# Four reorderings in a fused attention and feed-forward kernel: the start, one weight load, one output group, and the moment at which the next loads begin

## Chip, cores and metric

The kernel runs on one core of a Trainium2 chip. The metric is the device time of one execution in microseconds (us). A time is given as the median of several executions; a ratio is the mean time of one kernel's fast executions over the mean of the fast executions of the kernel before, taken in the same rounds on the same chip, so it is not quite the ratio of the medians quoted beside it. On one core an execution counts as slow when it is over 1.5% above the fastest of the same kernel.

Engine names as in the profile: PE is TensorE, DVE is VectorE, ACT is ScalarE, POOL is GpSimd, SP is SyncE. PEld is TensorE's loading of weights; SPq, ACTq and PEq are the engines' instruction queues; all DMAs of the page's list of issues come from SP's and POOL's. The span is the time from the first to the last instruction. The granted clock is the share of TensorE's full clock that the profile records as granted to it. POOL issues the loads from HBM that convert float32 to bfloat16; SP issues the DMA transposes and the stores.

## The reference, cut

```python
# q, k, v: [4, 8, 768, 64]; every row sees the first 8 keys and its last 96 keys
scores = q @ k^T / sqrt(64) - slope[h] * dist        # masked outside those keys
a = softmax(scores);  x = (a @ v) as [3072, 512]     # tokens x (heads * 64)
h = x @ w_in                                         # w_in  [512, 2048]
g = s * relu(h)**2 + b
out = g @ w_out                                      # w_out [2048, 512], float32 out
```

## The kernel before

The 3072 tokens are worked in 12 granules of 256. For granule `j`, `SS` computes scores and probabilities, `A` the attention output `xn[j]`, a transpose turns it into `xT[j]`, `P1` multiplies with `w_in` (8 groups of 8 matmuls) and `P2` with `w_out`. From granule 3 on everything is one software pipeline: period `j` holds the attention of `j`, `P1` of `j-1` and `P2` of `j-2` and `j-1`, and it loads granule `j+2`.

```python
    def pace(j):                       # POOL reads one element: its loads wait for it
        nc.gpsimd.tensor_copy(pdum[:], pts[j, 0][0:1, 0, 0:1])

    def load_granule(j):               # 2 + 2 + 2 DMAs of 128 KB, rows of 256 B in HBM
        load_rows(j, "k"); load_rows(j, "q"); load_v(j)

    def XT_dma(j):                     # two DMA transposes, 128 tokens each
        xT[j] = xpool.tile([P, KC, GT], BF16, name="xT", tag="xT")
        for i in range(GB):
            nc.sync.dma_start_transpose(xT[j][:, :, i * P : (i + 1) * P],
                                        xn[j][:, i, :, :].rearrange("p h d -> p (h d)"))
    # ... (cut)
    def period(j, items, at, late=None):
        SS(j, (0, 1))
        if j + 2 < NJ:
            pace(j)
            load_granule(j + 2)
        run(items, at[0])              # items: P1(j-1,0), P2(j-2,4), P1(j-1,1), ...
        A(j, 0)
        # ... (cut: A(j,1), SS(j,(2,3)), A(j,2), A(j,3) with items between)
        if late is None:
            XT_dma(j)                  # x transposes, then
        if j + 2 < NJ:
            XB(j + 2)                  # four transposes of k and q, on the same SP queue
        run(items, 100)                # the rest of P1 and P2
```

In the traces POOL's instructions run in the order of the program, and it has nothing else to do in the pipeline, so the tensor that `pace` reads, and not its place in the program, decides when the six loads begin (the timelines below show it: the copy after a wait of 10.63 us in before, then the loads 0.3 to 0.4 us after it). In before that is the first probabilities of granule `j`.

At the start, the first k and q arrive as float32 in two halves each (`raw32`, loaded by SP), are cast by DVE and ACT and transposed on PE. A POOL copy from `raw32` holds all of POOL's loads until the first k half has landed (in before it runs at 3.82 us, and the first v load follows at 4.20).

The softmax here doesn't subtract the row's maximum and nothing guards it: scores larger than these inputs give would overflow.

## Time and profile before

| | before |
|---|---|
| median of 4 executions, us | 219.19 (218.12 to 219.5) |
| profiled execution, us (span) | 223.86 (222.0), a slow one |
| PE busy | 95% of the span |
| one period, granules 4 to 6, us | 16.15 and 15.85 |
| x transpose, issue to landing, us | median 2.5, longest 5.8 |

The page of before: busy us of each engine, then the chain of work that ended last, by engine.

```profile
PE 210.5 (95%) x2027; PEld 141.7 (64%) x2027; DVE 135.8 (61%) x322; ACT 115.9 (52%) x176; POOL 69.1 (31%) x93
PE 74%; DMA 15%; DVE 4%; SPq 3%; ACT 2%; issue 1%
```

PE bounds the kernel, so time can only come from PE's idle time. The view of waits lists it: who waited for whom, us in total, times, longest.

```profile
PE ps L487 <- DMA xT<-xn: 2.1, 1, 2.1
PE ps_s L369 <- DMA qT<-qnat: 1.3, 1, 1.3
PE ps_t L263 <- DVE knat L155: 1.1, 1, 1.1
...
PE ps_t L263 <- DVE qnat L155: 0.5, 1, 0.5
```

The first line is a single stall, at 117 us. The chain in order of time (start, us, what) shows it: the x transpose of granule 6 took 5.65 us.

```profile
112.23 1.19 SPq L467
113.47 5.65 DMA xT<-xn
119.25 1.03 PE ps L487 x8
```

A usual period looks different. These are the timelines of SP, of POOL and of PE in before (start, us, engine, line, operation, out<-in, count).

```profile
80.23 2.50 SPq L467 DMA_TRANSPOSE xT<-xn  x2
82.82 2.52 SPq L294 DMA_TRANSPOSE kT<-knat  x2
```

```profile
86.94 0.18 POOL L124 COPY pdum<-pt 1x1 bf16<-1x1 bf16 x1 [10.63 <-DVE pt L386]
87.48 1.75 POOL L103 DMA_DIRECT2D knat<-in_k_dram  x2 [0.36 <-issue]
```

```profile
98.12 2.75 PE L530 MATMUL ps<-w_out_bf,gT 128*128 128x512 bf16 x12
100.81 0.51 PE L369 MATMUL ps_s<-qT,kT 64*128 64x128 bf16 x12
101.25 1.05 PE L487 MATMUL ps<-xT,w_in_bf 128*128 128x256 bf16 x8
```

The x transposes are issued at 80.23 and about 81.5 us and land 2.4 us after issue; the loads of the next granule start 7 us after the first of them; PE reaches the first P1 that needs them about 4.9 us after the first issue (here 101.25 for those issued at 96.38). The second transpose therefore has a slack of 1.1 to 1.2 us: it could land that much later before PE waits.

### The profile page before, as it was taken

The page shows a single profiled execution, that of the slowest core. Times are in us where ns is not written, and L with a number is a line of the kernel's source. Part 1 is how long each engine was busy: PE and PEld are TensorE (multiplying, and loading weights), DVE is VectorE, ACT ScalarE, POOL GpSimd, SP SyncE. Part 2 cuts the span into 40 slices and gives each one's busy share as a digit, 9 for nine tenths or more (in the row PEclk, how much of TensorE's full clock was granted, in tenths as well). Part 3 has the DMA queues.
Part 4 walks back from the last instruction along what each step waited for, and adds up shares of the span by engine and source line. Part 5 has one row for each costly group of instructions (what it writes and reads, how often), then busy time and mean ns, then how long its engine had stood idle before and what let it go on. Part 6 is the DMA issues. An engine that isn't in the chain of part 4 may idle for free.

```text
span 222.0 us, 4984 instructions
## 1 busy us (share of the span) xinstructions
PE 210.5 (95%) x2027; PEld 141.7 (64%) x2027; DVE 135.8 (61%) x322; ACT 115.9 (52%) x176; POOL 69.1 (31%) x93
## 2 busy tenths in 40 slices
PE   7779999999799999999996999999999999999993
PEld 2346877446566766766753676775776676675763
DVE  4565657699689676655754394664675675652431
ACT  6558899534557545544534445645544644641430
POOL 6966563450462702704505400810900000000000
PEclk9999999999999999999998899999999999999999
DMA  5999999999899996995997934995995322022102
GB/s 160 143 166 195 187 192 206 163 127 137 89 126 254 108 127 101 165 167 79 200 150 92 182 65 95 134 156 107 131 162 101 70 73 73 0 75 70 47 3 95
DMA packets 107207, 27.60 MB, mean 124 GB/s; under 512 B 95792, under 2 KB 104240, under 8 KB 107184
## 3 DMA queue, kind: packets, MB, share of 16 engines
q0 software_dynamic: 72896, 13.11, 80.6%
q1 hardware_dynamic: 34288, 14.17, 30.7%
q8 instruction: 16, 0.26, 0.5%
q14 instruction: 7, 0.06, 0.1%
HBM read 27.26 MB, written 6.29 MB: 151 GB/s over the span
## 4 chain that ended last, share of the span: by engine, by line
PE 74%; DMA 15%; DVE 4%; SPq 3%; ACT 2%; issue 1%
PE ps L487 32%; PE ps L530 28%; DMA knat<-in_k_dram 6%; PE ps_av L414 5%; PE ps_s L369 5%; DMA qT<-qnat 4%; DMA xT<-xn 3%; DMA raw<-in_k_dram 2%; PE ps_2e L581 2%; PE ps_2s L530 2%; SPq L294 1%; ACT gT L496 1%; DVE xn L423 1%; PE ps_s L353 1%; SPq L302 1%
## 5 line engine op out<-in xcount | busy, mean ns | idle before, releaser
L487 PE MATMUL ps<-xT,w_in_bf 128*128 128x256 bf16 x768 | 95.4, 274 | 2.6 <-DMA xT<-xn 2.1
L496 ACT ACTIVATE gT<-ps 128x512 bf16<-128x512 f32 x96 | 57.3, 598 | 62.6 <-PE ps L487 62.1
L487 PEld LDWEIGHTS <-w_in_bf 128*128 128x128 bf16 x768 | 73.6, 98 | 21.1 <-issue 3.6
L530 PE MATMUL ps<-w_out_bf,gT 128*128 128x512 bf16 x336 | 83.4, 381 | 0.0
L478 DVE TENSOR_TENSOR gT<-gT 128x512 bf16<-128x512 bf16 x96 | 39.9, 420 | 25.6 <-ACT gT L496 25.6
L382 ACT ACTIVATE pt<-ps_s 128x1024 bf16<-128x1024 f32 (+1 forms) x48 | 43.2, 952 | 21.0 <-PE ps_s L369 20.7
L530 PEld LDWEIGHTS <-gT 128*128 128x128 bf16 x368 | 33.7, 98 | 30.5 <-issue 0.3
L386 DVE TENSOR_TENSOR pt<-pt,tmpl 128x1024 bf16<-128x1024 bf16 (+1 forms) x40 | 26.1, 653 | 14.6 <-ACT pt L382 13.6
L124 POOL COPY pdum<-pt 1x1 bf16<-1x1 bf16 x7 | 1.7, 237 | 72.5 <-DVE pt L386 72.5
L111 POOL DMA_DIRECT2D vaug<-in_v_dram x24 | 21.5, 913 | 3.7 <-DMA w_out_bf<-in_moe_w_out_dram 3.0
L423 DVE TENSOR_TENSOR xn<-ps_av,rc 128x256 bf16<-128x256 f32 x48 | 20.4, 424 | 1.7
L541 DVE SCALAR_TENSOR_TENSOR o_sb<-ps,s_bc,bvec 128x512 f32<-128x512 f32 x18 | 13.5, 748 | 12.6 <-PE ps L530 12.6
L414 PEld LDWEIGHTS <-pt 128*128 128x128 bf16 x352 | 16.2, 98 | 6.7 <-DVE xn L423 2.3
L422 DVE RECIPROCAL rc<-ps_av 128x4 f32<-128x4 f32 x48 | 8.6, 180 | 16.8 <-PE ps_av L414 16.5
L414 PE MATMUL ps_av<-vaug,pt 128*128 128x65 bf16 x224 | 17.7, 194 | 0.6 <-DVE rc L422 0.3
L103 POOL DMA_DIRECT2D knat<-in_k_dram x18 | 15.8, 883 | 6.3 <-PE ps_av L414 1.9
L103 POOL DMA_DIRECT2D qnat<-in_q_dram x18 | 15.9, 897 | 0.8 <-issue 0.8
L369 PE MATMUL ps_s<-qT,kT 64*128 64x128 bf16 x224 | 12.6, 218 | 1.4 <-DMA qT<-qnat 1.3
L414 PE MATMUL ps_av<-vo,pt 128*128 128x65 bf16 x128 | 12.2, 195 | 0.0
L369 PEld LDWEIGHTS <-kT 64*128 64x128 bf16 x224 | 7.1, 94 | 7.6 <-issue 6.9
L369 PE MATMUL ps_s<-qT,ko 64*128 64x128 bf16 x128 | 8.0, 216 | 0.0
L530 PE MATMUL ps_2s<-w_out_bf,gT 128*128 128x512 bf16 x32 | 7.6, 379 | 0.0
(67 smaller groups left out, 105.1 us busy)
## 6 DMA issues: line engine op xcount, KB each, us to landing
out_dram<-o_sb SPq DMA_DIRECT2D x23, 256.0 KB, 3.0
vaug<-in_v_dram POOLq DMA_DIRECT2D x24, 128.0 KB, 6.1
knat<-in_k_dram POOLq DMA_DIRECT2D x18, 128.0 KB, 4.9
qnat<-in_q_dram POOLq DMA_DIRECT2D x18, 128.0 KB, 6.0
w_in_bf<-in_moe_w_in_dram POOLq DMA_DIRECT2D x8, 256.0 KB, 10.5
w_out_bf<-in_moe_w_out_dram POOLq DMA_DIRECT2D x4, 512.0 KB, 12.7
raw<-in_k_dram SPq DMA_DIRECT2D x2, 256.0 KB, 3.9
raw<-in_q_dram SPq DMA_DIRECT2D x2, 256.0 KB, 4.2
```

Source lines behind the costliest of these rows:

```text
L103: nc.gpsimd.dma_start(t[:, i, :, :], src[b, :, sb * P : (sb + 1) * P, :].rearrange("h p d -> p h d"))
L111: nc.gpsimd.dma_start(vaug[b][:, sb, :, 0:D], v[b, :, sb * P : (sb + 1) * P, :].rearrange("h p d -> p h d"),)
L369: nc.tensor.matmul(ps[:, hi, oc * P : (oc + 1) * P], lhsT=kt[r, :], rhs=qT[j][r, hp, i * P : (i + 1) * P], start=not biased, stop=not bias ...
L382: nc.scalar.activation(pt[:, :, 0:n], ps[:, :, 0:n], ACT.Exp, scale=QSCALE)
L386: nc.vector.tensor_tensor(pt[:, :, 0:n], pt[:, :, 0:n], m, ALU.mult)
L414: nc.tensor.matmul(av[:, i, hi, :], lhsT=pt[:, hi, c * P : (c + 1) * P], rhs=vv, start=n_ == 0, stop=n_ == len(ops) - 1,)
L423: nc.vector.tensor_tensor(xn[j][:, :, 2 * hp : 2 * hp + 2, :], av[:, :, :, 0:D], rc[:].to_broadcast((P, GB, 2, D)), ALU.mult,)
L478: nc.vector.tensor_tensor(gs, gs, gs, ALU.mult)
L487: nc.tensor.matmul(ps[:, i, :], lhsT=w_in_bf[:, kc, fc * P : (fc + 1) * P], rhs=xT[j][:, kc, :], start=(kc == 0), stop=(kc == KC - 1),)
L496: nc.scalar.activation(gs, ps[:], ACT.Relu)
L530: nc.tensor.matmul(po[j, tb], lhsT=gT[j][:, fc, tb * P : (tb + 1) * P], rhs=w_out_bf[:, fc, :], start=(fc == 0), stop=(fc == FC - 1),)
L541: nc.vector.scalar_tensor_tensor(out=o_sb[:], in0=po[j, tb], scalar=s_bc[:], in1=bvec[:], op0=ALU.mult, op1=ALU.add,)
```

## The change

The intent: shorten the start, bring the k rows of granule 3 forward, and start each granule's loads earlier so that they are over before the next x transposes.

```diff
     def pace(j):
-        nc.gpsimd.tensor_copy(pdum[:], pts[j, 0][0:1, 0, 0:1])
+        nc.gpsimd.tensor_copy(pdum[:], xn[j - 1][0:1, 0, H - 1, 0:1])
@@ start of POOL's loads
-    nc.gpsimd.tensor_copy(pdum[:], raw32[0:1, 0, 0, 0:1])
     load_v(0)
@@ more_loads
+        load_rows(3, "k")
         load_w_out(3)
-        load_rows(3, "k")
@@ start: scores 0 and 1 before the second key half
-    idle(1, "av")
+    idle(2, "av")
+    for hp in range(2):
+        S_mm(0, hp, True)
+        S_post(0, hp, True)
     T_mm(0, 1, "k")
# ... (cut: SB_mm(0, 2) and SB_mm(0, 3) one step earlier)
@@ x of granule 0 before q of granule 1
+    XT_half(0, 1, "dve", "av")
     T_mm(1, 0, "q")
-    XT_half(0, 1, "dve", "av")
# ... (cut: P1(0, 3), P1(0, 4), P1(0, 5) earlier, between A and x of granule 1)
# ... (cut: P2 of granule 1 before the last P2 parts of granule 0, so that
#      w_out's last quarter may land later)
@@ period
-        SS(j, (0, 1))
         if j + 2 < NJ:
             pace(j)
             load_granule(j + 2)
+        SS(j, (0, 1))
```

More of the change, by code (lines that the diff above doesn't have):

```diff
@@ L623 @@
     cast("q", 1)
-    for hp in range(2):
-        S_mm(0, hp, True)
-        S_post(0, hp, True)
     idle(1, "av")
+    SB_mm(0, 2)
     T_mm(0, 1, "q", "av", True)
@@ L631 @@
     more_loads()
-    SB_mm(0, 2)
+    SB_mm(0, 3)
     S_mm(0, 2, True)
@@ L635 @@
     A(0, 0, "pso")
-    SB_mm(0, 3)
     S_mm(0, 3, True)
@@ L673 @@
     A(1, 2)
+    P1(0, 3)
     A(1, 3, "pso")
-    P1(0, 3)
     XT_half(1, 0, "act", "av")
+    P1(0, 4)
     XT_half(1, 1, "dve", "pso")
-    P1(0, 4)
+    P1(0, 5)
     P1(1, 0)
@@ L682 @@
     P1(1, 2)
-    P1(0, 5)
     make_tmpl(3)
@@ L721 @@
     XB(4)
+    P2_sc(1, 0, 0)
+    P2_mm(1, 0, 0)
     wsum_part(0)
+    XT_pe(2, "act", "psh")
+    P2_mm(1, 0, 1)
+    wsum_part(1)
+    P2_mm(1, 0, 2)
     P2_mm(0, 0, 3)
-    XT_pe(2, "act", "psh")
-    wsum_part(1)
     P2_raw(0, 0)
+    wsum_part(2)
     P2_mm(0, 1, 3)
     P2_raw(0, 1)
-    wsum_part(2)
-    P2_sc(1, 0, 0)
-    for part in range(4):
-        P2_mm(1, 0, part)
+    P2_mm(1, 0, 3)
     P2_raw(1, 0)
```

## The prediction

In item 6 of the prediction a sentence on how the queues share the DMA engines is cut, since no run here shows it; the transpose's 5.9 us beside loads against 2.5 alone carry the item without it. The sum loses no term: it is -0.8, -0.3, -1.3 and +0.7 us as recorded (they add up to -1.7; the record says about -1.9).

> **What bounds the kernel.** TensorE. The page has PE busy 210.5 of 222.0 us (95%), with 74% of the chain of work that ended last; from 60 us on the timeline is nearly gapless, one period of about 16.1 us per granule. So only PE's idle time can be saved. The profiled execution is a slow one (223.9 us against 219.15): PE waited 2.1 us at 117 us for an x transpose (5.8 us to landing instead of 2.5), and the windows then show the granted clock at 0.65 and 0.50 for 4 us. Such a stall costs about 4.5 us (estimate: 223.9 - 219.15); I take it as absent from the usual run.
>
> The rest of PE's idle time: in the first 16 us gaps of 0.35, 1.06 (k half 1), 0.46 (q half 1), 0.72 (kT evacuation) and 0.43 us (qT evacuation), 0.35 us at 22.7 (last A of granule 1), and 1.28 us at 55.4 us (qT of granule 3).
>
> **Behind the start: the load stream.** From the DMA view: w_in part 0 lands at 15.5 us (first P1 starts 16.2), part 2 at 21.0 (its P1 21.06), part 4 at 23.7 (24.3). Compute and loads are level; moving compute alone would find loads missing.
>
> **What the change does**
>
> 1. The Pool copy that held the loads until raw k half 0 landed goes: first v load at about 2.6 instead of 4.2 us. From 6 to 10 us the DMA moves only 119 to 133 GB/s, so I expect the stream about 1 us earlier. Cost: raw k and q half 1 (6.55 and 7.34 us) land 0.3 to 0.8 us later.
> 2. Scores 0 and 1 before the second key half, one idle matmul (0.2 us) added, a bias (0.33 us) off the chain: offsets the later raw halves.
> 3. x half 1 before q of granule 1: q's evacuation (DVE, 0.68 us) no longer queues behind x's copy, first P1 about 0.5 us earlier.
> 4. P1 between the A's of granule 1 fills the 0.35 us gap.
> 5. k rows of granule 3 before w_out's last quarter (about 2.5 us of stream): kT issues some 3 us earlier, qT (9 us to landing) finds a shorter queue, the 1.28 us wait goes. Output matmuls are reordered so that w_out's last quarter may land later.
> 6. Steady state: loads of granule j+2 start when x of j-1 is ready, about 7 us earlier, together with the x transposes. Beside loads a transpose took 5.9 us (62.6 us), alone 2.5. [...]The second x transpose has about 1.1 us of slack before P1 and overlaps only the first loads: I expect 0 to 0.5 us of wait in each of 5 periods. In return loads end well before the next x transposes, which removes the stall seen at 117 us.
>
> Sum: start -0.8, item 4 -0.3, item 5 -1.3, steady state +0.7: about -1.9 us.
>
> **Predicted: 217.3 us, 8 in 10 within 215.4 to 220.5.** Faster by over 2%: 0.06; within 2%: 0.86; slower by over 2%: 0.08.
>
> **Shown right if:** first P1 at 15.2 to 15.8 us, no qT wait near 55 us, w_in part 0 landing near 14.5 us; x transposes 3 to 5 us to landing, P1's waits for them below 0.5 us each, period still near 16.1 us.
>
> **Wrong if** x transposes take near 6 us every period: PE then waits 2 us each time, the clock may drop, and the kernel is some 5% slower. Also if raw k half 1 is delayed by over 1.5 us; or if P1(0,5), moved up, outruns w_in part 5 (24.95 us).

## The result

The changed kernel is slower: 233.71 us (232.08 to 237.72, 4 executions) against 219.19 us, ratio 1.0647 with a 95% interval of 1.0564 to 1.073. Its profiled execution took 237.72 us and counts as slow, as does that of before; the clean pair of profiles comes from the first two experiments below.

After's page and its waits:

```profile
PE 214.8 (91%) x1996; PEld 144.2 (61%) x2028; DVE 136.6 (58%) x322; ACT 115.9 (49%) x176; POOL 68.9 (29%) x92
PE 75%; DMA 14%; DVE 3%; ACT 2%; issue 2%; SPq 2%; ACTq 0%
```

```profile
PE ps L486 <- DMA xT<-xn: 12.3, 5, 3.0
PE ps L529 <- issue: 1.0, 6, 0.2
PE ps_t L262 <- DVE knat L155: 0.8, 1, 0.8
```

PE waits for x five times instead of once, 12.3 us in all. The wait for qT of granule 3 (1.3 us) is gone. One period in detail, first POOL and then PE; the x transposes of this period were issued from 97.38 us on:

```profile
97.49 0.24 POOL L124 COPY pdum<-xn 1x1 bf16<-1x1 bf16 x1 [12.71 <-DVE xn L422]
98.03 1.76 POOL L103 DMA_DIRECT2D knat<-in_k_dram  x2 [0.30 <-issue]
```

```profile
101.81 0.51 PE L368 MATMUL ps_s<-qT,kT 64*128 64x128 bf16 x12
105.30 1.89 PE L486 MATMUL ps<-xT,w_in_bf 128*128 128x256 bf16 x8 [2.98 <-DMA xT<-xn]
```

The chain of after for the same stretch:

```profile
97.70 0.88 SPq L466
98.58 0.05 issue
98.63 6.62 DMA xT<-xn
105.25 0.05 issue
105.30 1.89 PE ps L486 x8
```

The second transpose took 6.62 us instead of 2.5. Of the 4.1 us more, about 1.2 us was slack and 2.98 us became a wait. And the damage continues: the eight matmuls of P1 took 1.89 us where before took 1.05. The windows of after (busy us of each engine, then granted clock, DMA share and GB/s) show why:

```profile
core 0: us, PE busy (x) PEld busy (x) DVE busy (x) ACT busy (x) POOL busy (x), PEclk, DMA share, GB/s
97.00:105.00 8.00, 5.26 (x42) 3.10 (x41) 4.00 (x8) 2.77 (x5) 5.50 (x7) 1.00 1.26 90
105.00:109.00 4.00, 3.48 (x15) 2.08 (x16) 0.43 (x1) 0.60 (x1) 0.00 (x0) 0.57 2.03 137
109.00:117.00 8.00, 7.95 (x87) 6.00 (x86) 5.38 (x15) 3.87 (x7) 0.00 (x0) 1.00 0.62 121
```

After the wait the granted clock is 0.50 for 3.41 us (105.23 to 108.64). In this execution four of the five waits (all but the first) were followed by such a dip. The five periods from the first x transposes of granule 4 to those of granule 9 took 99.35 us (78.83 to 178.18); with the old pace they take 80.44 us (77.00 to 157.44, run after_old_pace). Of the 18.9 us between, 12.3 us are waits; I ascribe the other 6.6 us to the four dips, which at half speed could cost up to 6.8 us (an estimate: four times half of 3.41). This is a slow execution of after. The fast profile of before_new_pace, which has the same new pace, shows the same: these periods took 96.61 us (78.42 to 175.03), 16.2 us more than with the old pace, of which 11.5 us are waits, with three dips.

### The profile page after: what moved, and what is told of

Same layout as the page of the kernel before. It is cut to its first block, busy times and chain, and to the rows that moved or that the text cites. A ratio compares the mean times of both kernels' runs of the same rounds, so it can differ in the third digit from the quotient of the medians.

```text
span 235.9 us, 4960 instructions
## 1 busy us (share of the span) xinstructions
PE 214.8 (91%) x1996; PEld 144.2 (61%) x2028; DVE 136.6 (58%) x322; ACT 115.9 (49%) x176; POOL 68.9 (29%) x92
## 4 chain that ended last, share of the span: by engine, by line
PE 75%; DMA 14%; DVE 3%; ACT 2%; issue 2%; SPq 2%; ACTq 0%
PE ps L486 33%; PE ps L529 24%; DMA xT<-xn 13%; PE ps_av L413 5%; PE ps_s L368 4%; PE ps_2s L529 3%; PE ps_t L262 2%; SPq L466 2%; PE ps_2e L580 1%; PE ps_s L352 1%; DMA raw<-in_k_dram 1%; ACT gT L495 1%; DVE xn L422 1%; ACT pt L381 1%; PE ps_x L452 0%
## 5 line engine op out<-in xcount | busy, mean ns | idle before, releaser
L486 PE MATMUL ps<-xT,w_in_bf 128*128 128x256 bf16 x768 | 98.1, 279 | 12.4 <-DMA xT<-xn 12.3
L486 PEld LDWEIGHTS <-w_in_bf 128*128 128x128 bf16 x768 | 74.8, 100 | 33.0 <-issue 12.4
L529 PE MATMUL ps<-w_out_bf,gT 128*128 128x512 bf16 x308 | 81.5, 391 | 2.1 <-issue 1.0
L529 PEld LDWEIGHTS <-gT 128*128 128x128 bf16 x368 | 34.4, 100 | 31.8 <-issue 2.1
L124 POOL COPY pdum<-xn 1x1 bf16<-1x1 bf16 x7 | 1.7, 249 | 73.8 <-DVE xn L422 73.8
```

The costliest lines, as they stand in the source:

```text
L486: nc.tensor.matmul(ps[:, i, :], lhsT=w_in_bf[:, kc, fc * P : (fc + 1) * P], rhs=xT[j][:, kc, :], start=(kc == 0), stop=(kc == KC - 1),)
L529: nc.tensor.matmul(po[j, tb], lhsT=gT[j][:, fc, tb * P : (tb + 1) * P], rhs=w_out_bf[:, fc, :], start=(fc == 0), stop=(fc == FC - 1),)
```

## The experiments

The stated theory: the whole loss comes from loads that run beside the x transposes. The rivals: the other reorderings, some other cost of early loads, or the clock by itself.

### after_old_pace: the pace of before in the changed kernel

```diff
-        nc.gpsimd.tensor_copy(pdum[:], xn[j - 1][0:1, 0, H - 1, 0:1])
+        nc.gpsimd.tensor_copy(pdum[:], pts[j, 0][0:1, 0, 0:1])
# and SS(j, (0, 1)) again ahead of pace and load_granule in period
```

> The changed kernel with one thing undone: the loads of granule j+2 again wait for the first probabilities of granule j, as before. My theory: the whole loss is the loads running beside the x transposes, so this run has no waits of PE for x over 0.5 us and takes 216.5 to 219 us. Rival: the reordering at the start and of the output matmuls costs part of the loss, then it stays above 222 us.

Measured: 218.74 us (216.82 to 219.58), before 219.83 us in these rounds, ratio 0.9956 (0.9901 to 1.0011). PE's waits for x fell to one of 0.2 us:

```profile
PE ps L486 <- DMA xT<-xn: 0.2, 1, 0.2
```

This one undone edit takes the whole loss away; the rest of the change is worth about 0.4%, and that is not clear of zero.

### before_new_pace: only the new pace, in the kernel before

The same edit of `pace` and `period` as in the change, and nothing else of it.

> The kernel before with that one thing alone: loads of granule j+2 begin when x of granule j-1 is ready. My theory: 231 to 236 us, five waits of PE for x of 2 to 3 us, second x transpose 5 to 7 us to landing. Rival (the loss needs the other reorderings too, for instance a granule 5 load that comes earlier in the stream): below 226 us.

Measured: 235.11 us (234.49 to 236.61), ratio 1.0728 (1.0669 to 1.0788). The profiled execution is a fast one. Its waits:

```profile
PE ps L487 <- DMA xT<-xn: 9.7, 4, 3.0
PE ps L487 <- ACT pt L382: 1.8, 1, 1.8
```

The second line is a P1 too. This view names the engine whose signal came last by its record; here the second x transpose was also in flight. It landed at 145.82 us and P1 began at 145.96, 0.14 us later, as in most of the waits that the view gives to x; so I count it as a fifth wait for x (the same holds for such lines in k_only_early, big_packets_early and gate_back). The new pace is enough for the loss without any of the reorderings.

### pace_landed: the loads held until the transposes have landed

```diff
-        nc.gpsimd.tensor_copy(pdum[:], xn[j - 1][0:1, 0, H - 1, 0:1])
+        nc.gpsimd.tensor_copy(pdum[:], xT[j - 1][0:1, 0, P : P + 1])
```

> The changed kernel with the loads of granule j+2 held until the second x transpose of granule j-1 has landed, about 4 us after x is ready instead of 0.5 us. If the loss comes from loads and x transposes being in flight together: both x transposes land in about 2.5 us, PE waits for none of them, 215.5 to 218.5 us. If early loads cost something by themselves ([...]the k and q transposes behind them), it stays above 222 us.

Measured: 218.34 us (216.39 to 218.57), ratio 0.9939 (0.9888 to 0.9989). No wait for x is left. POOL's timeline shows the loads about 4.4 us after the issue of the x transposes (77.03) instead of 0.6:

```profile
80.87 0.18 POOL L124 COPY pdum<-xT 1x1 bf16<-1x1 bf16 x1 [9.29 <-DMA xT<-xn]
81.41 1.75 POOL L103 DMA_DIRECT2D knat<-in_k_dram  x2 [0.36 <-issue]
```

Early loads are harmless here once they do not overlap the transposes that PE is about to need. The k and q transposes behind them still overlap (issued from 79.61 and 82.31 us, the loads from 81.41), but PE needs those over a period later: no wait for them is in the list. The x transposes of granule 6 still took up to 4.4 us, which the slack absorbed; I did not find why that granule is special. Under the old pace the stall of before can come back: the profile of gate_back has a wait of 1.83 us at granule 6, those of after_old_pace and w_out_first 0.2 us or none. In before the last load of granule 8 landed at 115.30 us, 3.1 us after the first x transpose of granule 6 was issued; one period earlier this overlap was 1.3 us.

### idle_fill: keep PE busy through the wait

```diff
         SS(j, (0, 1))
+        if 5 <= j <= 9:
+            idle(10, "av")      # ten matmuls of ones, no useful work
```

> The changed kernel with ten matmuls of ones (about 2.2 us of TensorE at full clock) in front of the first input matmul of granules 4 to 8, where PE waits for x. They are no useful work. If the lower granted clock after each wait follows from TensorE being idle, the clock stays near 1.0, the waits left are below 1 us each, and the time falls by 3 to 7 us against the changed kernel, to 226 to 231 us. If the clock falls for another reason, the time stays at 232 to 236 us with the clock near 0.98.

Measured: 229.93 us (229.26 to 230.32), ratio 1.0479 (1.0429 to 1.0529), mean granted clock 1.0 and one wait of 0.5 us left. The wait at the same place as above:

```profile
101.87 2.36 PE L228 MATMUL ps_i<-const-bfloat16-1.0 128*128 128x512 bf16 x9
104.75 1.05 PE L486 MATMUL ps<-xT,w_in_bf 128*128 128x256 bf16 x8 [0.52 <-DMA xT<-xn]
```

P1 takes 1.05 us again. Useless work made the changed kernel 3.8 us faster (233.71 to 229.93), because PE kept its clock (1.00 in all windows from 97 to 131 us, where after has 0.57 from 105 to 109). The 11.2 us left above after_old_pace are about the five fills (2.36 us for the one above). So the loss has two parts, the waits and the lower clock that follows them.

The traces also show which waits cost the clock. In the traces of after, before, before_new_pace and k_only_early nine of the eleven waits for x of 2.0 to 3.0 us were followed by a clock of 0.50 for 3.41 us, and so was one of 1.90 us (after); the waits of 2.34 us (after) and 2.07 us (before_new_pace) were not, nor was one of 1.83 us in gate_back. Within one trace the dips begin a multiple of 3.41 us apart (in after at 105.23, 125.71, 146.19 and 166.67 us). I cut these four traces into stretches of 3.41 us on that grid, after and before from 20 us on, the other two from 82 to 175 us. Every stretch in which PE was idle for 1.90 us or more was followed by a dip, and none with 1.82 us or less was. The wait of 2.34 us in after, which cost no clock, fell on two stretches (0.9 and 1.5 us of idle time). The grid lies differently in each execution (the dip of before at 120.59 us is 4.5 stretches from the first of after), which would explain why after has four dips and before_new_pace three for five waits each. What sets the grid is not shown.

### late_p1 and its control late_p1_old_pace: give the transposes more time

```diff
-[(P1,m,0), (P2,l,4), (P1,m,1), (P2,l,5), (P1,m,2), (P2,l,6), (P1,m,3), (P2,l,7)]
+[(P2,l,4), (P2,l,5), (P2,l,6), (P2,l,7), (P1,m,0), (P1,m,1), (P1,m,2), (P1,m,3)]
```

> The changed kernel, early loads kept, with the four output matmul groups of granule j-2 moved ahead of the first input matmul group of granule j-1, which gives the x transposes about 3.5 us more. The x transposes still take 5 to 7 us to land. If the loss is only that TensorE waits for them in order, the waits are below 0.5 us and the time is 216 to 220 us. If early loads slow the kernel in another way too, it stays above 223 us.

Measured: 225.16 us (224.09 to 225.26), ratio 1.0262 (1.0225 to 1.0299). The time is what I wrote for the rival, but its profile is not: the second x transposes still took up to 6.8 us and no wait for x was left, while other waits had come, in periods without loads too:

```profile
PE ps L529 <- DVE o_sb L540: 2.7, 8, 0.4
PE ps L486 <- ACT gT L495: 2.7, 6, 0.4
```

P2 now comes to its tile `ps` before DVE has read it out (8 waits, 2.7 us in all), and the P1 groups in a row come to theirs before ACT has (6 waits, 2.7 us). The control puts the old pace under the same order.

> Control for late_p1 (225.16 us): the same order of matmul groups with the loads begun at the old time. If early loads cost nothing beside the waits for x, this takes the same time as late_p1, 223.5 to 226 us, because the order itself costs two waits of 0.3 to 0.4 us in every period. If early loads cost more than that, this is faster by over 2 us.

Measured: 225.54 us (224.37 to 225.55), ratio 1.0264 (1.0219 to 1.0308), with the same waits:

```profile
PE ps L486 <- ACT gT L495: 3.2, 6, 0.8
PE ps L529 <- DVE o_sb L540: 2.7, 8, 0.4
```

Under this order the early loads cost nothing that can be measured: 1.0262 against 1.0264, each within about 0.4%. What was left in late_p1 is the order's own price. So early loads hurt, as far as these runs can tell, only through the P1 that PE reaches too soon.

### k_only_early: two of the six loads early

`pace` on `xn[j - 1]` before the two k loads, a second copy from `pts[j, 0]` before the q and v loads.

> The changed kernel with only the two k loads begun with the x transposes and the q and v loads at the old time. My prediction said that the second transpose meets only the first loads; if these two are enough to slow it, it still takes 5 us or more and the time stays above 226 us. If the whole queue of six behind them makes the delay, it takes about 4 us, the waits are below 0.5 us each and the time is below 221 us.

Measured: 232.6 us (229.72 to 235.09), ratio 1.0569 (1.0509 to 1.0628). The second transposes that PE waited for took up to 6.4 us, and the waits are:

```profile
PE ps L489 <- DMA xT<-xn: 8.8, 4, 2.8
PE ps L489 <- ACT pt L384: 1.8, 1, 1.8
```

The first two loads are enough for nearly the whole loss. That is the assumption of my prediction (only the first loads overlap) with the opposite consequence.

### big_packets_early: the same bytes in long rows

after_old_pace plus, for `5 <= j <= 9`, a copy from `xn[j - 1]` and two loads of 128 KB of `w_out` rows (2 KB each in HBM) into a tile that nothing reads.

> The run after_old_pace plus two loads of 128 KB that nothing reads, begun when x of granules 4 to 8 is ready: the same bytes as the two early k loads of k_only_early, but in 128 rows of 2 KB instead of 1024 rows of 256 B. If the delay of the x transposes comes from the number of small packets, they now land in under 3.5 us, PE waits under 0.5 us for each, and the time is 217 to 221 us. If it comes from the bytes or from any load being there, they take 5 us or more and the time is 226 us or more.

Measured: 222.92 us (221.33 to 223.51), ratio 1.0146 (1.0096 to 1.0196), second x transposes of granules 4 to 8 landing about 4 us after issue, up to 5.6, waits of 0.5 to 2.1 us. This lies between the two expectations. The size of the rows matters, since two loads of 1024 short rows cost about 13.9 us over after_old_pace (232.6 against 218.74) and two of 128 long ones 4.2 us for the same bytes, but long rows are not free. (Each such load reads 256 KB of float32; the 128 KB count the bfloat16 that arrives. The long-row loads come on top of the usual six, the early k loads do not.) POOL also issues a long-row load faster (0.56 against 0.88 us), so the two are not placed quite alike in time. What exactly slows the transposes inside the DMA engines stays open.

### gate_back: the hold at the start

after_old_pace with `nc.gpsimd.tensor_copy(pdum[:], raw32[0:1, 0, 0, 0:1])` put back before the first load.

> The changed kernel with the old pace and with the Pool copy back that holds the first loads until raw k half 0 has landed; the rest of the change stays. If the earlier stream is worth the 1 us I predicted, this is about 1 us slower than the run after_old_pace in its ratio to before (0.9956), so about 1.000. If [...]holding it back is as fast or faster: ratio 0.990 to 0.996, first cast 0.43 us.

Measured: 217.82 us (216.99 to 219.1), ratio 0.9945 (0.991 to 0.998); the first cast took 0.43 us. Against after_old_pace (0.9956, other rounds) there is no difference outside the intervals. The earlier stream is not worth the 1 us that I gave it, and the ratio and the cast are those of my second alternative. What was seen is that the first cast takes 0.84 us in after against 0.43 in before. The long first cast does go with the missing hold, though not always: of the ten profiles without the hold eight have it (0.84 us in after, 0.90 in after_old_pace, 0.86 in w_out_first; in all eight PE waits 0.77 or 0.78 us for it and starts its first transposes at 4.69 or 4.70 us), and pace_landed and landed_idle9 cast in 0.43. Of the four with the hold none has it (0.43 us in before, gate_back and before_landed; in before_new_pace PE starts those transposes at 4.21 us). Why is not shown.

### landed_idle9: no gap before the first transposes

pace_landed with `idle(9, "av")` instead of `idle(7, "av")` as the very first work.

> The run pace_landed with nine instead of seven idle matmuls at the very start, so that TensorE has no gap between 3.9 and 4.7 us. Executions of the changed kernels fall into two groups about 2 us apart (216.4 and 216.7 against 218.3 to 218.6 in pace_landed), and a profile of the slower kind has the matmuls from 4.7 to 9.5 us at half speed. If that gap decides whether the clock is up in time, nearly all executions are now in the faster group: 216 to 217 us, ratio 0.985 to 0.990. If it is chance alone, the two groups stay and the ratio is 0.993 or worse.

Measured: 217.06 us (216.67 to 217.8), ratio 0.9906 (0.9877 to 0.9936). The slowest execution is 217.8 us, where four of the six of pace_landed were above 218.3; but three of the six lie above 217, the ratio falls between my two expectations, and its interval overlaps that of pace_landed. PE's first us in after, then in this run:

```profile
0.77 3.15 PE L228 MATMUL ps_i<-const-bfloat16-1.0 128*128 128x512 bf16 x7 [0.77 <-PEq L839]
4.70 0.64 PE L262 MATMUL ps_t<-ident,knat 128*64 128x128 bf16 x8 [0.78 <-DVE knat L155]
5.27 1.46 PE L352 MATMUL ps_s<-base,diag 128*128 128x384 bf16 x4
```

```profile
0.78 3.95 PE L228 MATMUL ps_i<-const-bfloat16-1.0 128*128 128x512 bf16 x9 [0.78 <-PEq L839]
4.65 0.41 PE L262 MATMUL ps_t<-ident,knat 128*64 128x128 bf16 x8
5.00 0.82 PE L352 MATMUL ps_s<-base,diag 128*128 128x384 bf16 x4
```

In after the same matmuls take 1.46 instead of 0.82 us, until about 9.5 us, and the first P1 starts at 16.79 us instead of 15.00. The granted clock does not show this: the windows of after read 1.00 from 4.70 to 9.50 us, where the trace has no clock record yet (its first is at 9.66 us; that of before at 4.54). Only the durations of the matmuls show it. The gap of 0.78 us, which comes with the long first cast, does not always have this effect: of the eight profiles with it six start at half speed, and those of after_old_pace and big_packets_early run at full speed (0.82 us for the matmuls above). The grid of 3.41 us, counted back from the dips, may bear on it too: the first clock record, at 9.66 us in after and 4.54 us in before, lies on a point of it in both, and from about there PE is at full speed (in before the transposes from 4.27 us on take 0.52 us, the same matmuls from 4.73 us on 0.82). After_old_pace is fast with the gap, so the one profile of landed_idle9 may have been fast with the gap too; that closing the gap is what helped is not shown. This is the lowest ratio of all versions, about 1% below before; the intervals of pace_landed, gate_back and before_landed overlap with it.

### w_out_first and before_landed: what the rest of the change is worth

w_out_first is after_old_pace with `load_w_out(3)` again ahead of `load_rows(3, "k")`.

> The run after_old_pace with the last quarter of w_out again ahead of the k rows of granule 3. As I predicted, the wait of 1.28 us for qT of granule 3 near 55 us should come back (0.8 to 1.8 us) and the time rise by about that, to a ratio of 1.000 to 1.004. If the earlier start alone had removed it, there is no such wait.

Measured: 218.93 us (218.37 to 219.51), ratio 0.9983 (0.9933 to 1.0033), and no wait for qT. The profile had the slow kind of start, so PE reached the scores of granule 3 only at 55.15 us; qT landed there near 54.7 us (second issue about 45.8, 8.8 us to landing). In after_old_pace, with the fast start, PE was there at 53.41 and qT had landed near 52.8 us. So with a fast start about 1.3 us of wait would be back (an estimate, 54.7 minus 53.4, if qT lands no earlier then); the run itself does not show it.

before_landed is before with the pace of pace_landed.

> The kernel before with only the hold of the loads changed, to the landing of the second x transpose of granule j-1. The stall at granule 6, seen in the profile of before, should be gone and the time be 216.5 to 218.5 us, ratio 0.990 to 0.997. Against pace_landed (0.9939) it shows what all the reordering at the start and of w_out is worth: I expect it slower than pace_landed by 0.3 to 0.8% (rival: no difference, the reordering is worth nothing).

Measured: 218.41 us (217.12 to 219.13), ratio 0.9946 (0.9906 to 0.9987). The long stall is gone from its profile, with the longest x transpose at 4.3 us. Against pace_landed (0.9939) nothing is left for the reorderings: the rival holds, as long as the start may run slowly. Against landed_idle9 (0.9906) the difference is 0.4%, within the intervals.

## Why the prediction was wrong, point by point

- **The step that failed is number 6**, "The second x transpose has about 1.1 us of slack before P1 and overlaps only the first loads: I expect 0 to 0.5 us of wait in each of 5 periods." The slack was right (1.2 us), and so was the effect, that a transpose slows down beside loads. The size was not: the second transposes took 5.4 to 6.6 us, the waits were 1.9 to 3.0 us in every one of the 5 periods (5.3 to 6.6 and 1.8 to 3.0 us in the fast profile of before_new_pace), and two loads alone (k_only_early) do nearly all of it. The step did not even fit its own forecast of 3 to 5 us to landing: 5 us, minus 2.5 us and the slack, is a wait of 1.4 us. The sum carried +0.7 us for the steady state; the change of pace alone measured +15.3 us (before_new_pace, 235.11 against 219.83 us).
- The trace of before held the right number. A transpose (of k) beside loads took 5.9 us at 62.6 us, and the stall at 117 us was such a collision too, beside the last loads of granule 8 and a store (5.65 us, 2.1 us of wait, then a lower clock). I quoted both and then scaled the first down for an overlap that I had only argued. Taken as measured, 5.9 us minus 2.5 us minus 1.2 us of slack gives 2.2 us per period.
- "Wrong if" named what came: transposes near 6 us, 2 us of wait each time, a lower clock and some 5% (measured 6.5%). I gave it too little weight. The lower clock stood only there and not in the sum; it is about 3.8 us of the loss (idle_fill).
- "In return loads end well before the next x transposes" came true and bought little: the stall that it removes occurs once, while five new ones were made. pace_landed removes the first without making the others.
- Item 1: w_in part 0 landed at 14.8 us instead of 15.5, raw k half 1 at 6.85 and raw q half 1 at 8.00 us. The delays were as predicted. The stream came 0.7 us earlier in after, but 0.9 us earlier with the hold put back (14.6 us, gate_back), so the gain cannot be put down to the hold; and its worth in time is not measurable.
- Items 2 and 3: with a fast start the first P1 begins at 14.8 to 15.0 us instead of 16.16, better than predicted; with the slow start at 16.4 to 16.8 us. I had not foreseen that, so where it came out better than predicted, that is partly luck.
- Item 4: the gap of 0.35 us at 22.7 us is gone (a new one of 0.26 us stands at 13.25 us).
- Item 5: the wait for qT is gone, as predicted; that the order of the k rows did it is not shown.
- All items but 6 together: -2.4 us predicted, about -1 us measured (after_old_pace), not clear of zero.

## What to carry to other kernels

When a transfer that PE needs soon has about 1 us of slack, do not start a bulk of loads beside it; wait for its landing, which here cost one tiny copy on the issuing engine (0.18 us) and was worth 15 us (233.71 against 218.34). Take a measured collision at its measured length, and add the clock that PE may lose after a wait as long as those here (1.9 to 3.0 us, ten of twelve in four traces followed by 3.41 us at 0.50): in the fast profile of before_new_pace 11.5 us of waiting went with 16.2 us lost. After moving work at the start, look at the durations of PE's first matmuls: six of the eight profiles with a gap of 0.78 us there ran at half speed for several us.
